# Loading later x tiles already transposed and centring them on GpSimd

## The chip, the cores and the metric

The kernel runs on one core of one Trainium2 chip. The metric is device time in microseconds (us) for one execution, and lower is better. In what follows PE is TensorE, DVE is VectorE, ACT is ScalarE, POOL is GpSimd, and SP is the engine that issues most of the DMAs. A difference of 0.2% is 1.3 us here.

## The reference

A layer normalisation of x (2048 tokens, 512 features) feeds two parallel mixers, whose results are added to x. Cut to what matters:

```python
xn = layernorm(x)                                  # (x - mean) / sqrt(var + 1e-5), per token
# A: linear attention, 32 heads of 16
q, k, v = split(xn @ wqkv)
phi_q, phi_k = [softmax(p), softmax(-p)] of p = q @ w_phi and of p = k @ w_phi, per head
o = phi_q (phi_k^T v) / (phi_q phi_k^T 1)
# B: gated MLP over the sequence
z = gelu(xn @ w_in);  z1, z2 = halves of z;  z2 = layernorm(z2)
out = x + o @ wo + (z1 * (w_sp @ z2 + b_sp)) @ w_out
```

## The kernel before

The 2048 tokens are 16 tiles of 128. Products run as three passes of float32r parts (`mm3`, lines 51 to 53: high times high, high times low, low times high), so every operand is split into a high part (ACT rounds it, line 43) and a rest (DVE subtracts, line 47).

The change lies in the first stage, about the first 217 us. For each tile `s` the stage does this:

1. `fetch(s)` has SP load the tile, tokens on the partitions (`xt`, line 168, 256 KB). Five such buffers are used in turn, and the blocks of `w_in` (`wst_`, line 179) use the same five.
2. `stats(s)`: DVE takes mean and variance (lines 234 and 236). POOL makes the negative mean `nm` (line 237) and the reciprocal deviation `r_x` (lines 84 and 85).
3. `center(s)`: ACT adds `nm` to the tile, one value per partition (line 242).
4. `transposed(s)`: PE transposes the tile in four blocks into a PSUM tile `pt` (line 248), so that features lie on the partitions.
5. `split_x`: ACT and DVE split `pt` into `xT[s]` (lines 43 and 47).
6. PE multiplies `xT[s]` by the weights: V (`proj`, evicted to `v` by ACT, line 257), K and Q (`proj`, read by DVE, lines 103 to 113, with an exponential on ACT, line 110), and the first half of the gated MLP (`zps`, evicted to `z1f` by ACT, line 139).
7. `add_kv`: DVE scales K's features `e` (line 269), POOL issues a DMA that adds them into `zacc` (line 270), and PE adds to the K-V product (`kvps`, line 273). Q's features go to DRAM (`e_d`, line 265, a DMA that POOL issues).

`proj` and `pt` share four PSUM buffers, `zps` has two. K's `e` has two buffers. Each engine runs its own instructions strictly in order; the order is set when the program is built, by a scheduler that takes instructions as they become ready in its own simulated time. So an edit to a step can move instructions of other steps. Tiles 0 to 2 are handled by lines written out in a fixed order ahead of the loop, and tiles 3 to 15 by `centered(s + 2)` in the loop.

An input `x_t` that holds x with each tile transposed already exists, and this kernel does not read it.

After the first stage come the second half of the gated MLP (to about 290 us), the product with `w_sp` (`g`), and a last stage with the output projections; the change does not touch their code.

Of the kernel before, what the change touches and what calls it, by code (L numbers as in the profile page):

```python
# [10 lines left out]
F32 = mybir.dt.float32  # L11
F32R = mybir.dt.float32r
AF = mybir.ActivationFunctionType
ALU = mybir.AluOpType
# [4 lines left out]
P = 128  # L19
S, D, H, DH, FH = 2048, 512, 32, 16, 688  # L20
NT = S // P
ND = D // P
# [13 lines left out]
def mixer(ctx: ExitStack, tc: tile.TileContext, x, x_t, wv, wqkT, phi_bd, wo, w_in, wst, b_r, w_out, out):  # L36
    nc = tc.nc
    pe, act, dve, pool, sp = nc.tensor, nc.scalar, nc.vector, nc.gpsimd, nc.sync


    def round_h(eng, h, src):
        if eng is act:
            return act.activation(h, src, AF.Copy).ins  # L43
        return eng.tensor_copy(h, src).ins

    def rest_l(l, src, h, eng=None):
        return (eng or dve).tensor_tensor(l, src, h.bitcast(F32), op=ALU.subtract).ins  # L47
# [18 lines left out]
    dram = ctx.enter_context(tc.tile_pool(name="dram", bufs=1, space=DRAM))  # L66
# [2 lines left out]
    u_d = dram.tile([NT, P, FH + REM], F32, name="u_d")  # L69
    kvT_d = dram.tile([P, D], F32, name="kvT_d")  # L70
    zb_d = dram.tile([P, NF], F32, name="zb_d")

    ident = cst.tile([P, P], F32, name="ident")
    make_identity(nc, ident)
# [6 lines left out]
    def rstd_of(mv, r, stats=None):  # L81
        if stats is not None:
            dve.bn_aggr(mv, stats)
        pool.tensor_scalar_add(mv[:, 1:2], mv[:, 1:2], EPS_LN)
        pool.tensor_tensor(r, mv[:, 1:2], mhalf, op=ALU.pow)
# [36 lines left out]
    def zproj(ps, s, w, order=(0, 1)):  # L122

        if ps in (za, kv_ps_p):
            p = [ps.tile([P, D], F32, tag="z", name="zps") for _ in range(2)]
        else:
            q = ps.tile([P, 2, D], F32, tag="z", name="zps")
            p = [q[:, k] for k in range(2)]
        t = xT[s]
        for k, j in enumerate(order):  # L130
            for c in range(ND):
                cs = slice(c * P, (c + 1) * P)
                mm3(p[k][:, :FC], (t[:, 0, cs], t[:, 1, cs]), (w[j][0][:, c], w[j][1][:, c]), c == 0, c == ND - 1)
        return [(slice(k, k + 1), p[k][:, :FC].unsqueeze(1)) for k in range(2)] if ps in (za, kv_ps_p) else [(slice(0, 2), q[:, :, :FC])]

    def z1_raw(pl, ps, s, bufs):
        z = pl.tile([P, 2, FC], F32, tag="zf", bufs=bufs, name="z1f")
        for k, p in zproj(ps, s, w1):
            act.activation(z[:, k], p, AF.Copy, scale=r_x[:, s:s + 1])
        act.dma_start(z1_d[s], z.rearrange("p a b -> p (a b)"))  # L140
# [20 lines left out]
    with ExitStack() as p0:  # L161
        res = p0.enter_context(left("p0res", 1))
        wk = p0.enter_context(left("p0wk", 2))
        ps = p0.enter_context(psum("p0ps", 4))

        def load_x(s):
            t = wk.tile([P, D], F32, tag="x", bufs=XB, name="xt")
            sp.dma_start(t, x[s * P:(s + 1) * P, :])
            return t
# [15 lines left out]
        def load_rows(src, x_at={}):  # L185
            raw = [stage("wrow") for _ in range(2)]
            parts = [raw[c // 2][:, c % 2, :D] for c in range(ND)]
            for c in range(ND):
                if c in x_at:
                    fetch(x_at[c])  # L190
                sp.dma_start(parts[c], src[c * P:(c + 1) * P, :])
            return parts
# [15 lines left out]
        def load_win(dst, j, stp, tag, bufs):  # L208
            for c in range(ND):
                t = stp.tile([P, D if tag == "x" else FC], F32, tag=tag, bufs=bufs, name="wst_")  # L210
                split_w(dst[0][:, c], dst[1][:, c], w_in[c * P:(c + 1) * P, j * FC:(j + 1) * FC], t[:, :FC])

        def proj(s, wh, wl):
            p = ps.tile([P, D], F32, tag="mm", name="proj")
            for c in range(ND):
                cs = slice(c * P, (c + 1) * P)
                proj.last = mm3(p, (xT[s][:, 0, cs], xT[s][:, 1, cs]), (wh[:, c], wl[:, c]), c == 0, c == ND - 1)
            return p

        xt, v = {}, {}  # L220

        def fetch(s):
            if s < NT:
                xt[s] = load_x(s)

        def split_x(src):
            t = xz.tile([P, 2, FH], F32R, tag="xz", name="xT")
            xT.append(t)
            src = src.rearrange("p a b -> p (a b)")
            return round_h(act, t[:, 0, :D], src), rest_l(t[:, 1, :D], src, t[:, 0, :D])  # L230

        def stats(s):
            st6 = wk.tile([P, 6], F32, tag="st6", name="st6")
            dve.bn_stats(st6, xt[s])
            nm = wk.tile([P, 1], F32, tag="nm", name="nm")
            ins = dve.bn_aggr(mv_x[:, s], st6).ins
            pool.tensor_scalar_mul(nm, mv_x[:, s, 0:1], -1.0)
            rstd_of(mv_x[:, s], r_x[:, s:s + 1])
            return nm, ins

        def center(s, nm):
            return act.activation(xt[s], xt[s], AF.Identity, bias=nm).ins

        def transposed(s):
            xs = xt.pop(s)
            pt = ps.tile([P, ND, P], F32, tag="mm", name="pt")
            for c in range(ND):
                ins = pe.transpose(pt[:, c], xs[:, c * P:(c + 1) * P], ident).ins  # L248
            return pt, ins

        def centered(s):
            center(s, stats(s)[0])
            split_x(transposed(s)[0])

        def proj_v(s):
            v[s] = wk.tile([P, D], F32, tag="v", name="v")
            ins = act.activation(v[s], proj(s, wv_h, wv_l), AF.Copy, scale=r_x[:, s:s + 1]).ins
            return proj.last, ins

        def proj_k(s):  # L260
            return softmax_pair(wk, proj(s, wqk_h[:, 1], wqk_l[:, 1]), "k", r_x[:, s:s + 1])

        def proj_q(s):
            e = softmax_pair(wk, proj(s, wqk_h[:, 0], wqk_l[:, 0]), "q", r_x[:, s:s + 1])
            pool.dma_start(e_d[s], e)

        def add_kv(s, er):
            vs, e = v.pop(s), er[:, :NF]
            dve.tensor_tensor(heads(e), heads(e), bc(er[:, NF:], 2 * H), op=ALU.mult)
            pool.dma_start(zacc, e, accum_op=ALU.add)  # L270
            for m in range(H // 2):
                k = m % 4 * QP
                pe.matmul(kv_acc[k:k + QP, m // 4], vs[:, m * QP:(m + 1) * QP], e[:, m * HP:(m + 1) * HP],  # L273
                          start=s == 0 and m < 4, stop=s == NT - 1, skip_group_check=True)
# [3 lines left out]
        wvr = load_rows(wv, {2: 1})  # L278
        fetch(2)
        wqT = load_rows(wqkT[:D])  # L280
        fetch(3)
        sp.dma_start(bias, b_r)


# [11 lines left out]
        with ExitStack() as queue:  # L296
# [3 lines left out]
            nm, i = stats(0)  # L300
# [9 lines left out]
            nm, i = stats(1)  # L310
# [8 lines left out]
            p = proj(0, wqk_h[:, 1], wqk_l[:, 1])  # L319
# [5 lines left out]
            nm, i = stats(2)  # L325
# [13 lines left out]
                    proj_v(1)  # L339
        n1 = nq = 0  # L340
        for s in range(NT):
            fetch(s + 4)
            er = proj_k(s) if s else ek
            if 0 < s < NT - 2:
                centered(s + 2)
            while nq < (s - 2) * NT // (NT - 3):
                proj_q(nq)
                nq += 1
            add_kv(s, er)
            if s + 2 < NT:  # L350
                proj_v(s + 2)
            if s == 1:
                for j in range(2):
                    load_win(w1[j], j, wk, "x", XB)
            while n1 < s * (NT - LAG) // (NT - 1):
                z1_raw(wk, za, n1, 2)
                n1 += 1
# [18 lines left out]
    def q_fin(et, tmp, zb):  # L376

        e, r, t, w = et[:, :NF], *(et[:, NF + k * 2 * H:NF + (k + 1) * 2 * H] for k in range(3))
        den = et[:, NF + 6 * H:QW]
        dve.tensor_tensor(tmp, e, zb, op=ALU.mult)  # L380
        dve.tensor_reduce(t, heads(tmp), axis=AX.X, op=ALU.add)
        dve.tensor_tensor(t, t, r, op=ALU.mult)
        dve.scalar_tensor_tensor(den, pairs(t, 0), EPS_DEN, pairs(t, 1), op0=ALU.add, op1=ALU.add)
        dve.reciprocal(den, den)
        dve.tensor_tensor(w.rearrange("p (h a) -> p h a", a=2), r.rearrange("p (h a) -> p h a", a=2),
                          den.unsqueeze(2).to_broadcast([P, H, 2]), op=ALU.mult)
        return e, dve.tensor_tensor(heads(e), heads(e), bc(w, 2 * H), op=ALU.mult).ins
# [46 lines left out]
    with ExitStack() as p1:  # L434
# [39 lines left out]
        for s in range(NE):  # L474
            et = load_q(s, tb.tile([P, QW], F32, tag="et", bufs=2, name="et"))
            tmp = zw.tile([P, 4, FC], F32, tag="z2", bufs=2, name="qtmp").rearrange("p a b -> p (a b)")[:, :NF]
            e, _ = q_fin(et, tmp, zb)
# [11 lines left out]
    nb = 0  # L489
# [44 lines left out]
    for s in range(NT):  # L534
        p = zproj((kv_ps_p, zc, zbp, za)[s % 4], s, w2, (0, 1) if s % 2 == 0 else (1, 0))
# [171 lines left out]
    wk = ctx.enter_context(left("cwk", 2))  # L707
# [82 lines left out]
    p = {0: project_u(0, uT.pop(0))}  # L790
# [20 lines left out]
    for i in range(0, NT, 2):  # L811
        if i:
# [3 lines left out]
            with tc.issue_after(lasts[2]):  # L816
                oT, _ = attend(fT)
# [49 lines left out]
```

## Time and profile before

| | |
|---|---|
| median of 3 runs | 654.72 us (654.68 to 655.67) |
| span of the profiled execution | 651.5 us, so 3.2 us of the median lie outside a span like this one; no other time of that execution is given |
| PE busy | 644.0 us (99% of the span) |
| DVE, ACT, POOL busy | 509.3, 279.4 and 96.6 us |
| granted TensorE clock | 1.000 |
| DMA | 98.36 MB, mean 151 GB/s |

Busy time of PE counts from the start of a matmul to its modelled end, and matmuls overlap; the distance from one start to the next is what one costs. In the chain of work that ended last, each piece has its start, its length on the chain and what it is. A list of waits names the waiting instruction first, then what released it, then the total, the number of times and the longest.

### The profile page before, as it was taken

The page shows a single profiled execution, that of the slowest core. Times are in us where ns is not written, and L with a number is a line of the kernel's source. Part 1 is how long each engine was busy: PE and PEld are TensorE (multiplying, and loading weights), DVE is VectorE, ACT ScalarE, POOL GpSimd, SP SyncE. Part 2 cuts the span into 40 slices and gives each one's busy share as a digit, 9 for nine tenths or more (in the row PEclk, how much of TensorE's full clock was granted, in tenths as well). Part 3 has the DMA queues.
Part 4 walks back from the last instruction along what each step waited for, and adds up shares of the span by engine and source line. Part 5 has one row for each costly group of instructions (what it writes and reads, how often), then busy time and mean ns, then how long its engine had stood idle before and what let it go on. Part 6 is the DMA issues. An engine that isn't in the chain of part 4 may idle for free.

```text
span 651.5 us, 10927 instructions
## 1 busy us (share of the span) xinstructions
PE 644.0 (99%) x4163; PEld 580.2 (89%) x4163; DVE 509.3 (78%) x921; ACT 279.4 (43%) x464; POOL 96.6 (15%) x185
## 2 busy tenths in 40 slices
PE   7999999999999999999999999999999999999997
PEld 6888888888888999999999999999999777787885
DVE  4988987998889578989977869678696588989321
ACT  5644334342333438887443434434452432233220
POOL 3332221101101014441010010010100000001000
PEclk9999999999999999999999999999999999999999
DMA  8365344544444951002353352433557867864610
GB/s 307 78 161 138 100 130 103 149 124 113 124 141 144 302 164 65 2 2 78 129 187 128 124 171 89 163 122 115 177 182 269 290 210 265 295 237 165 214 50 32
DMA packets 38884, 98.36 MB, mean 151 GB/s; under 512 B 4688, under 2 KB 6736, under 8 KB 38832
## 3 DMA queue, kind: packets, MB, share of 16 engines
q1 hardware_dynamic: 27632, 56.77, 26.7%
q0 software_dynamic: 8896, 35.26, 17.8%
q10 hardware_dynamic: 2304, 5.64, 2.3%
q8 instruction: 32, 0.52, 0.3%
q14 instruction: 20, 0.16, 0.1%
HBM read 56.37 MB, written 26.61 MB: 127 GB/s over the span
## 4 chain that ended last, share of the span: by engine, by line
PE 97%; DMA 1%; DVE 0%; ACT 0%; SPq 0%; issue 0%; POOL 0%; POOLq 0%
PE g L53 11%; PE g L52 11%; PE g L51 11%; PE proj L53 7%; PE proj L51 7%; PE proj L52 7%; PE zps L53 6%; PE zps L52 6%; PE zps L51 6%; PE pout L51 5%; PE pout L53 5%; PE pout L52 5%; PE po L761 2%; PE kvps L273 1%; PE ptq L749 1%; PE pt L248 1%
## 5 line engine op out<-in xcount | busy, mean ns | idle before, releaser
L53 PE MATMUL g<-B,A 128*128 128x344 f32 x448 | 143.3, 320 | 0.0
L52 PE MATMUL g<-B,A 128*128 128x344 f32 x448 | 143.2, 320 | 0.0
L51 PE MATMUL g<-B,A 128*128 128x344 f32 x448 | 143.2, 320 | 0.0
L51 PEld LDWEIGHTS g<-B,A 128*128 128x128 f32 x448 | 84.2, 188 | 0.0
L53 PEld LDWEIGHTS g<-B,A 128*128 128x128 f32 x448 | 84.2, 188 | 0.0
L52 PEld LDWEIGHTS g<-B,A 128*128 128x128 f32 x448 | 84.1, 188 | 0.0
L47 DVE TENSOR_TENSOR A<-S,A 128x512 fp32r<-128x512 f32 x64 | 43.7, 688 | 33.4 <-ACT A L43 32.5
L43 ACT ACTIVATE A<-S 128x512 fp32r<-128x512 f32 x64 | 40.0, 631 | 58.5 <-PE g L53 36.3
L110 ACT ACTIVATE e<-e,r_x 128x1024 f32<-128x1024 f32 x32 | 36.8, 1152 | 43.8 <-DVE e L109 43.1
L51 PE MATMUL proj<-wqk_h,xT 128*128 128x512 f32 x128 | 51.4, 401 | 0.3 <-ACT wqk_h L43 0.3
L52 PE MATMUL proj<-wqk_l,xT 128*128 128x512 f32 x128 | 50.5, 394 | 1.1 <-DVE wqk_l L47 1.1
L43 ACT ACTIVATE A<-wf 128x512 fp32r<-128x512 f32 x64 | 33.4, 522 | 41.1 <-PE g L53 40.4
L53 PE MATMUL proj<-wqk_h,xT 128*128 128x512 f32 x128 | 50.9, 397 | 0.0
L51 PE MATMUL zps<-w_0h,xT 128*128 128x344 f32 x128 | 41.8, 326 | 0.0
L112 DVE TENSOR_REDUCE sm<-e 128x64 f32<-128x1024 f32 x32 | 38.6, 1208 | 3.3 <-ACT e L110 3.3
L53 PE MATMUL zps<-w_0h,xT 128*128 128x344 f32 x128 | 41.1, 321 | 0.0
L51 PE MATMUL zps<-w_1h,xT 128*128 128x344 f32 x128 | 41.0, 320 | 0.0
L53 PE MATMUL zps<-w_1h,xT 128*128 128x344 f32 x128 | 41.0, 320 | 0.0
L52 PE MATMUL zps<-w_0l,xT 128*128 128x344 f32 x128 | 40.9, 320 | 0.0
L52 PE MATMUL zps<-w_1l,xT 128*128 128x344 f32 x128 | 40.9, 319 | 0.0
L47 DVE TENSOR_TENSOR A<-wf,A 128x512 fp32r<-128x512 f32 x64 | 35.4, 553 | 3.9 <-ACT A L43 3.4
L751 ACT ACTIVATE f<-ptq 128x512 f32<-128x512 f32 x32 | 16.5, 603 | 34.7 <-PE ptq L749 27.8
(193 smaller groups left out, 1439.9 us busy)
## 6 DMA issues: line engine op xcount, KB each, us to landing
wf<-in_wst SPq DMA_DIRECT2D x64, 256.0 KB, 3.4
e_d<-e POOLq DMA_DIRECT2D x16, 544.0 KB, 5.2
et<-e_d SPq DMA_DIRECT2D x16, 544.0 KB, 4.9
zacc<-e POOLq DMA_DIRECT2D x16, 512.0 KB, 4.9
er<-et POOLq DMA_DIRECT2D x12, 512.0 KB, 4.6
u_d<-z1t POOLq DMA_DIRECT2D x16, 368.0 KB, 4.4
u<-u_d SPq DMA_DIRECT2D x15, 368.0 KB, 4.6
z_d<-z1f ACTq DMA_DIRECT2D x16, 344.0 KB, 3.4
```

The costliest lines, as they stand in the source:

```text
L43: return act.activation(h, src, AF.Copy).ins
L47: return (eng or dve).tensor_tensor(l, src, h.bitcast(F32), op=ALU.subtract).ins
L51: pe.matmul(dst, ah, bh, start=start, stop=False)
L52: pe.matmul(dst, ah, bl, start=False, stop=False)
L53: return pe.matmul(dst, al, bh, start=False, stop=stop).ins
L110: act.activation(e, e, AF.Exp, scale=scale)
L112: dve.tensor_reduce(sm, heads(e), axis=AX.X, op=ALU.add)
L248: ins = pe.transpose(pt[:, c], xs[:, c * P:(c + 1) * P], ident).ins
L273: pe.matmul(kv_acc[k:k + QP, m // 4], vs[:, m * QP:(m + 1) * QP], e[:, m * HP:(m + 1) * HP], start=s == 0 and m < 4, stop=s == NT - 1, ski ...
L749: pe.transpose(pt[:, a, k].bitcast(F32R), src, ident_r)
L751: act.activation(f, pt.rearrange("p a k b -> p a (k b)"), AF.Copy)
L761: lasts[3] = pe.matmul(po[g // 2][a * HP:(a + 1) * HP, g % 2], kvT[:, 2 * g + a], fs[g][:, a], start=True, stop=True).ins
```

## The change

Tiles 3 to 15 are no longer centred by ACT and transposed by PE. Each is loaded twice: once as before (for mean and variance alone), and once from `x_t`, transposed, into `xc` (two buffers, 256 KB each). Since a token's mean now belongs to a column and not to a partition, POOL issues a DMA that writes the 128 values of `nm` to a row in DRAM, SP issues a DMA that reads that row back into all 128 partitions (`nb`, two buffers, 64 KB), and POOL adds `nb` to `xc`, 128x512 elements. `split_x` then reads `xc`.

```diff
+    nm_d = dram.tile([NT, P], F32, name="nm_d")
...
-        def centered(s):
-            center(s, stats(s)[0])
-            split_x(transposed(s)[0])
+        xc = {}
+
+        def load_xT(s):
+            if s >= NT:
+                return
+            fetch(s)
+            xc[s] = wk.tile([P, ND, P], F32, tag="xc", bufs=2, name="xc"), wk.tile([P, P], F32, tag="nb", bufs=2, name="nb")
+            sp.dma_start(xc[s][0], x_t[s])
+
+        def center_T(s):
+            if s >= NT:
+                return
+            nm, _ = stats(s)
+            xt.pop(s)
+            t, nb = xc[s]
+            pool.dma_start(nm_d[s:s + 1, :].rearrange("a p -> p a"), nm)
+            sp.dma_start(nb, nm_d[s:s + 1, :].to_broadcast([P, P]))
+            pool.tensor_tensor(t, t, nb.unsqueeze(1).to_broadcast([P, ND, P]), op=ALU.add)
...
-        fetch(3)
+        load_xT(3)
...
-            fetch(s + 4)
+            load_xT(s + 4)
+            if s == 0:
+                center_T(3)
             er = proj_k(s) if s else ek
             if 0 < s < NT - 2:
-                centered(s + 2)
+                split_x(xc.pop(s + 2)[0])
+                center_T(s + 3)
```

The scheduler places the new instructions, and this is seen on three queues. First POOL, about 30 us into the program. Before, `nm_594` is the negative mean of tile 5, `nm_722` that of tile 6, and `e_249` and `e_375` are K's features of tiles 0 and 1:

```order
L237 TENSOR_SCALAR nm_594<-mv_x_76 128x1
L84 TENSOR_SCALAR mv_x_76<-mv_x_76 128x1
L85 TENSOR_TENSOR r_x_77<-mv_x_76,mhalf_73 128x1
L270 DMA zacc_94<-e_249 128x1024
L270 DMA zacc_94<-e_375 128x1024
L237 TENSOR_SCALAR nm_722<-mv_x_76 128x1
```

After, `xc_142`, `xc_328` and `xc_376` are the transposed tiles 3, 4 and 5, `nm_513` is the negative mean of tile 5, and `e_253` K's features of tile 0:

```order
L269 TENSOR_TENSOR xc_142<-xc_142,nb_143 128x512
L238 TENSOR_SCALAR nm_513<-mv_x_77 128x1
L85 TENSOR_SCALAR mv_x_77<-mv_x_77 128x1
L267 DMA nm_d_68<-nm_513 128x1
L86 TENSOR_TENSOR r_x_78<-mv_x_77,mhalf_74 128x1
L269 TENSOR_TENSOR xc_328<-xc_328,nb_329 128x512
L269 TENSOR_TENSOR xc_376<-xc_376,nb_377 128x512
L286 DMA zacc_95<-e_253 128x1024
```

The additions now stand between the statistics and ahead of the DMA into `zacc`, and the mean of tile 5 is taken only behind the addition of tile 3.

Second ACT, at the splits of the first tiles of the loop. Before, `xT_395` and `xT_501` are tiles 3 and 4, `v_342` is V of tile 2, and `e_375` and `e_481` are K's features of tiles 1 and 2:

```order
L43 ACTIVATE xT_395<-pt_390 128x512
L257 ACTIVATE v_342<-proj_343,r_x_77 128x512
L110 ACTIVATE e_375<-e_375,r_x_77 128x1024
L139 ACTIVATE z1f_537<-zps_538,r_x_77 128x344
L43 ACTIVATE w1_1h_112<-wst__455 128x344
L43 ACTIVATE w1_1h_112<-wst__459 128x344
L43 ACTIVATE xT_501<-pt_496 128x512
L242 ACTIVATE xt_463<-xt_463,nm_722 128x512
```

After, `xc_328`, `xc_376`, `xc_482` and `xc_586` are tiles 4 to 7, `e_395` and `e_501` K's features of tiles 1 and 2, and `v_359` and `v_433` V of tiles 2 and 3:

```order
L43 ACTIVATE xT_508<-xc_328 128x512
L43 ACTIVATE xT_612<-xc_376 128x512
L111 ACTIVATE e_395<-e_395,r_x_78 128x1024
L140 ACTIVATE z1f_554<-zps_555,r_x_78 128x344
L273 ACTIVATE v_359<-proj_360,r_x_78 128x512
L111 ACTIVATE e_501<-e_501,r_x_78 128x1024
L140 ACTIVATE z1f_554<-zps_556,r_x_78 128x344
L43 ACTIVATE xT_740<-xc_482 128x512
L141 DMA z1_d_64<-z1f_554 128x688
L43 ACTIVATE xT_838<-xc_586 128x512
L273 ACTIVATE v_433<-proj_434,r_x_78 128x512
```

The splits have moved forward by several tiles: tile 5 is split ahead of the exponential of K of tile 1, and tile 7 ahead of the eviction of V of tile 3.

Third SP, in the same stretch. Before, only loads of x follow each other there; after, `nb_483` and `nb_587` are the broadcasts of tiles 6 and 7, and `xt_1316` and `xt_1444` the plain loads of tiles 13 and 14:

```order
L259 DMA xc_482<-in_x_t 128x512
L259 DMA xc_586<-in_x_t 128x512
L268 DMA nb_483<-nm_d_68 128x128
L169 DMA xt_1316<-in_x 128x512
L169 DMA xt_1444<-in_x 128x512
L268 DMA nb_587<-nm_d_68 128x128
```

A broadcast now stands behind loads that wait for a buffer, and loads of later tiles behind broadcasts that wait for a write to DRAM.

## The prediction

> **What bounds the kernel now.** I read the page first (span, engines, chain), then PE's waits, then the stage windows, then the groups that the change touches.
>
> ```profile
> span 651.5 us, 10927 instructions
> PE 644.0 (99%) x4163; PEld 580.2 (89%) x4163; DVE 509.3 (78%) x921; ACT 279.4 (43%) x464; POOL 96.6 (15%) x185
> PE 97%; DMA 1%; DVE 0%; ACT 0%; SPq 0%; issue 0%; POOL 0%; POOLq 0%
> ```
>
> The chain is PE from end to end. PE's waits and the windows (columns: window, then busy us of PE, PEld, DVE, ACT, POOL, then clock, DMA share, GB/s) say where it is not full:
>
> ```profile
> PE idle L293 <- POOL ident masks.py:199: 1.8, 1, 1.8
> PE proj L52 <- DVE wqk_l L47: 1.1, 1, 1.1
> PE proj L51 <- ACT wqk_h L43: 0.3, 1, 0.3
> ...
> 31.00:60.00 29.00, 29.00 (x233) 24.68 (x233) 25.33 (x42) 14.44 (x22) 9.97 (x20) 1.00 0.53 128
> 60.00:100.00 40.00, 40.00 (x313) 33.39 (x312) 34.25 (x53) 15.86 (x21) 7.99 (x16) 1.00 0.52 138
> 100.00:200.00 100.00, 100.00 (x693) 84.20 (x692) 86.59 (x124) 36.36 (x45) 14.10 (x23) 1.00 0.43 123
> 217.00:240.00 23.00, 23.00 (x142) 22.00 (x141) 14.37 (x28) 12.51 (x24) 0.00 (x0) 1.00 0.84 277
> ```
>
> All of PE's waits are in the start; from 31 us on it has none, at clock 1.00. So work taken off PE there shortens the span one for one, as long as nothing else makes PE wait. DVE is next, at 85 to 87% of the stage that changes.
>
> **What is removed from PE.** The transposes of 13 tiles, four matmuls each. In the chain the first and the last of these 13 pieces, and one with its neighbours:
>
> ```profile
> 30.67 0.44 PE pt L248 x4
> ...
> 177.71 0.44 PE pt L248 x4
> ```
>
> ```profile
> 72.31 0.23 PE proj L53
> 72.55 0.44 PE pt L248 x4
> 72.98 0.16 PE zps L53
> 73.14 0.16 PE zps L51
> ```
>
> ```profile
> L248 PE MATMUL pt<-ident,xt x52: 270/272/273, 30.5 to 177.9; 128*128 128x128 f32 x52
> ```
>
> 52 is 13 times 4. The neighbours keep their steps of 0.23 and 0.16, so no changeover hides around a piece. 13 x 0.44 = 5.7 us. This is the main term, and all of it is on the path.
>
> **What is removed or cheaper elsewhere.** ACT loses 13 centrings, and the splits read SBUF instead of PSUM:
>
> ```profile
> L242 ACT ACTIVATE xt<-xt,nm 128x512 f32<-128x512 f32 x16 | 11.5, 722 | 22.5 <-POOL nm L237 22.5
> L43 ACT ACTIVATE xT<-pt 128x512 fp32r<-128x512 f32 x16 | 9.6, 598 | 21.8 <-PE pt L248 21.8
> L43 ACT ACTIVATE A<-wf 128x512 fp32r<-128x512 f32 x32 | 20.1, 628 | 26.3 <-PE g L53 25.6 <-ACT A L43 0.4 <-DMA wf<-in_wst 0.3
> L47 DVE TENSOR_TENSOR xT<-pt,xT 128x512 fp32r<-128x512 f32 x16 | 10.8, 678 | 2.5 <-ACT xT L43 2.5
> L47 DVE TENSOR_TENSOR A<-wf,A 128x512 fp32r<-128x512 f32 x32 | 22.0, 686 | 2.9 <-ACT A L43 2.8
> ```
>
> ACT is freed 13 x 0.72 = 9.4 us; it is half idle in this stage, so this is worth nothing by itself. The same split from SBUF (`wf`) takes 628 and 686 ns, against 598 and 678 from PSUM: no gain. Also `pt` no longer takes one of the four PSUM buffers, which lets PE run further ahead of DVE. I count that as zero, since PE never waits there.
>
> **What is added.** For each of 13 tiles: one addition on POOL, one tiny DMA issued by POOL, one broadcast and one 256 KB load issued by SP. The nearest rows:
>
> ```profile
> L154 POOL TENSOR_TENSOR mask<-mask 128x128 f32<-128x128 f32 x1 | 0.5, 455 | 0.1
> L76 POOL MEMSET mhalf<- 128x1 f32 x1 | 0.1, 98 | 0.0
> L265 POOL DMA_DIRECT2D e_d<-e x16 | 9.2, 574 | 21.9 <-DVE e L113 8.4 <-issue 5.0 <-DVE e L108 4.2
> ...
> e_d<-e POOLq DMA_DIRECT2D x16, 544.0 KB, 5.2
> xt<-in_x SPq DMA_DIRECT2D x16, 256.0 KB, 4.6
> out<-xr SPq DMA_DIRECT2D x16, 256.0 KB, 2.1
> wst__431<-in_w_in SPq DMA_DIRECT2D x1, 172.0 KB, 2.3
> ```
>
> The addition has four times the elements of the `mask` addition: between 98 + 4 x (455 - 98) ns = 1.53 us and 4 x 455 ns = 1.82 us; I take 1.5, since a fixed part is not repeated. With 0.6 us for the DMA's issue POOL gets 13 x 2.1 = 28 us more, and it is 14 to 34% busy in the windows above. The DMAs add 13 x (256 + 64) KB = 4.2 MB; over the 70 us or so in which the walk below places them that is 60 GB/s, beside the 128 to 138 that are moved at half load. Neither engine is near full.
>
> The landing of the tiny write and of the broadcast is shown nowhere. The nearest rows go from 2.1 us (a 256 KB store) to 5.2 us (the 544 KB that POOL issues). I take 2.7 for the write and 2.2 for the broadcast, nearer the lower end, since the longer times are of more bytes; 4.9 together, 10.4 at the upper end. The Trainium skill, "DMA: Bandwidth & Descriptors", section "Specifications", says that pieces below 512 B make the engine read, modify and write; the write here is of 4-byte pieces, and no run here shows one. By that rule its time would lie higher in this range.
>
> **Is a tile ever late?** The order sets the question: ACT holds V of tile 3 (`v_433`) behind the split of tile 7, and ACT waits in order. `v_433` frees the PSUM buffer that V of tile 5 takes on PE. Durations for the walk:
>
> ```profile
> L110 ACT ACTIVATE e<-e,r_x 128x1024 f32<-128x1024 f32 x32 | 36.8, 1152 | 43.8 <-DVE e L109 43.1 <-ACT z1f L139 0.7
> L257 ACT ACTIVATE v<-proj,r_x 128x512 f32<-128x512 f32 x16 | 10.9, 682 | 10.4 <-PE kvps L273 10.3
> 42.45 0.58 PE kvps L273 x32
> 43.03 0.43 PE proj L53
> ```
>
> PE: from 30.7 us, where tile 3's transposes were, it has ahead of V of tile 5 five products of V, K and Q (60 `proj` matmuls x 0.23), the first half of the gated MLP for two tiles (48 x 0.157) and two `kvps` (0.58 each, and the `proj` behind one takes 0.43 instead of 0.23): 13.9 + 7.5 + 1.6 = 23.0. So V of tile 5 is due at 53.7.
>
> POOL and SP, by the prices above: tile 3's mean is written by 23, broadcast by 25, added by 26.7. POOL takes tile 5's mean only then: written by 30, broadcast by 32; its `xc` is loaded when tile 3's split has freed the buffer, and lands by 35; added by 36.5, split by 38.5. That frees tile 7's buffer; its broadcast is issued at about 43.5 behind loads of x, and lands by 45.7; POOL has means and a DMA in between and adds at 46.6 to 48.1. ACT splits (0.6) and evicts V of tile 3 (0.7): 49.4. That is 4.3 us ahead of need. Tiles 8 to 11 come out the same way at 3 to 6 us each, one to four us ahead. So at my prices PE never waits, and the whole 5.7 remain. If the cover is gone, the evictions of V and `z1f` are late next, and PE waits on PSUM.
>
> With both landings at 5.2 us, tile 7 is added at 52.6, just in time; tile 8, whose mean POOL takes behind tile 6, is 1.9 us late at the eviction of V of tile 4; tiles 10 and 11 make `z1f` another 3.7 late. That is 5.7 us: exactly the gain.
>
> **At the start**, the two extra 256 KB loads stand ahead of the first `w_in` block; its row on the chain:
>
> ```profile
> 15.31 2.27 DMA wst__431<-in_w_in
> 19.93 0.66 PE pt L248 x4
> ```
>
> ```profile
> GB/s 307 78 161 138 100 130 103 149 124 113 124 141 144 302 164 65 2 2 78 129 187 128 124 171 89 163 122 115 177 182 269 290 210 265 295 237 165 214 50 32
> ```
>
> Two loads at the 307 GB/s of the first slice cost up to 1.7 us, but DVE now takes tile 2's mean ahead of that block's rest, which returns 0.5 to 1.0. I count zero, with 0.5 either way. Behind the stage, PE is full too (217 to 240 above), so a gain is passed on to the end.
>
> **Sum.** 651.5 - 5.7 = 645.8 us of span; on the median of the runs, whose 3.2 us outside the span don't change, 654.7 - 5.7 = 649.0.
>
> **One contention, weighed.** POOL's and DVE's rows at one place:
>
> ```profile
> 46.38 1.23 DVE L269 TENSOR_TENSOR e<-e 128x1024 f32<-128x1024 f32 x1
> ...
> 46.54 1.14 POOL L84 TENSOR_SCALAR mv_x<-mv_x 128x1 f32<-128x1 f32 x1
> ```
>
> POOL's smallest operation took 1.14 us and ended with DVE's. So the two seem to shut each other out, and an addition of 1.5 us could hold DVE in turn. Six additions fall in 31 to 60 us; at 0.6 us each they take 3.7 us, which is all the idle time that DVE has there (29.0 - 25.3). The Trainium skill, "SBUF — State Buffer", section "Who interferes with whom", says that a DVE instruction with two SBUF inputs and a GpSimd instruction that reads SBUF exclude each other for a whole instruction. By that rule the split and the scaling of `e` are held; the trace agrees with the 1.14 us.
>
> **The rivals.**
> - Full gain (above), 648.2 to 650.5: 0.50.
> - Part of it lost: DVE held as just worked out and PE losing up to 3.7 us, or landings between my prices and the upper end: 650.5 to 653.4. Chance 0.24.
> - The round trip eats the gain, landings near 5.2 us each: 653.4 to 656.0, no change that a measurement could tell. Chance 0.12.
> - Slower: the round trip of the mean, in ACT's order. It decides from 10.4 us for write and broadcast together; each further us is paid again at tiles 8, 10, 12 and 14, whose splits stand ahead of evictions, so at 11.5 us about 5.7 + 4 x 1.1 = 10 us of waits: 659. Against it speaks that it needs more than twice my price. Chance 0.14.
> - That the transposes remain is excluded: only those of tiles 0 to 2 are left in the program.
>
> **Numbers.** Faster 0.74, same 0.12, slower 0.14. The likeliest is 649.0. The range 648.2 to 656.0 leaves out the slower case and little below the full gain.
>
> **What would show it.** Right: 12 transposes left, no PE wait behind 31 us, the span near 646, POOL's addition 1.5 us, the broadcast's landing near 2. Wrong: ACT's `xT` waiting on POOL's `xc` and PE on ACT's `v` or `z1f` between 38 and 80 us; or a write to `nm_d` that lands after more than 5 us.

## The result, and the profile after

The changed kernel takes 704.62 us (median; 702.49 to 708.76) beside 654.7 us for the kernel before (654.5 to 655.67): a ratio of 1.0768, 95% interval 1.073 to 1.0806. It is slower by 50 us. The forecast of 649.0 us was wrong, and so was its range.

The head of the page after, and the engines' line of the chain:

```profile
span 700.8 us, 10907 instructions
PE 648.1 (92%) x4111; PEld 580.3 (83%) x4111; DVE 509.1 (73%) x921; ACT 269.7 (38%) x451; POOL 120.5 (17%) x211
PEclk9989785999999999999999999999999999999999
PE 78%; DMA 1%; DVE 1%; issue 0%; ACT 0%
```

The chain can be followed back only to 139.5 us here, so its shares say nothing of the stage before that. The 52 transposes are gone (4163 matmuls before, 4111 now), and yet PE is busy for longer, and no longer for the whole span. PE's longest waits after (what waited, what released it, total us, times, longest):

```profile
PE zps L51 <- ACT z1f L140: 18.0, 2, 16.3
PE proj L51 <- ACT v L273: 15.9, 3, 9.7
PE proj L51 <- ACT xT L43: 5.3, 1, 5.3
PE proj L51 <- DVE e L110: 4.5, 3, 2.6
```

The windows after show where (window, busy us of PE, PEld, DVE, ACT and POOL, then clock, DMA share, GB/s):

```profile
20.00:40.00 20.00, 14.69 (x66) 11.93 (x65) 11.89 (x23) 8.66 (x17) 7.69 (x13) 0.85 0.68 99
...
60.00:80.00 20.00, 10.31 (x99) 7.99 (x99) 10.76 (x20) 2.27 (x4) 7.60 (x14) 0.74 0.43 93
80.00:100.00 20.00, 14.56 (x93) 11.79 (x91) 9.66 (x16) 4.46 (x6) 7.48 (x12) 0.91 0.80 92
100.00:120.00 20.00, 4.03 (x13) 3.64 (x14) 7.34 (x11) 4.79 (x7) 9.06 (x16) 0.57 0.30 58
120.00:140.00 20.00, 16.36 (x104) 13.08 (x103) 9.94 (x15) 4.56 (x7) 7.60 (x6) 1.00 0.80 151
...
160.00:180.00 20.00, 20.00 (x150) 16.19 (x149) 18.96 (x29) 5.81 (x7) 3.38 (x5) 1.00 0.44 122
20.00:160.00 140.00, 96.06 (x623) 78.01 (x622) 80.99 (x131) 36.82 (x56) 48.10 (x75) 0.87 0.58 106
```

From 20 to 160 us PE stands idle for 140 - 96.1 = 43.9 us, where before it had no wait at all. The granted clock is lower there too: 0.57 in the 20 us in which PE works for 4.03. Three matmuls, the last ahead of a wait of 5.3 us and the first two behind it (start, us, instruction, idle time before it and what released it):

```profile
30.07 0.40 PE L53 MATMUL proj<-wv_h,xT 128*128 128x512 f32 x1
35.77 0.79 PE L51 MATMUL proj<-wv_h,xT 128*128 128x512 f32 x1 [5.31 <-ACT xT L43]
36.37 0.63 PE L52 MATMUL proj<-wv_l,xT 128*128 128x512 f32 x1
```

After each of PE's four longest waits (5.2 to 16.3 us) the matmuls of 128x512 take 0.63 us in place of 0.39, for 3 to 5 us; after the waits of 1.8 and 2.6 us they don't. From 160 us on PE is full again. In the 80 to 100 us row the DMA engines are busy for 0.80 of the time and move 92 GB/s; at 0.80 again, from 120 to 140 us, they move 151. Busy, then, is not the same as moving.

The waits behind PE's, and the DMAs of the first 260 us (KB each, median us to landing):

```profile
ACT xT L43 <- POOL xc L269: 73.6, 11, 13.5
POOL xc L269 <- DMA xc<-in_x_t: 29.2, 6, 11.8
POOL xc L269 <- DMA nb<-nm_d: 20.5, 2, 11.4
POOL nm L238 <- DMA nm_d<-nm: 19.4, 4, 8.3
...
xc<-in_x_t SPq DMA_DIRECT2D x13, 256.0 KB, 5.4
nb<-nm_d SPq DMA_DIRECT2D x13, 64.0 KB, 5.0
nm_d<-nm POOLq DMA_DIRECT2D x13, 0.5 KB, 8.3
wst__464<-in_w_in SPq DMA_DIRECT2D x1, 172.0 KB, 8.8
```

The write of 512 bytes takes longer than the loads of 256 KB (over the whole run 7.2 to 14.6 us). Five of the eight blocks of `w_in` in this stage take 4.2 to 8.8 us; before, six took 2.2 or 2.3 and the other two 4.1 and 4.8. POOL itself waits for the write four times: the buffer of `nm` is free for a new mean only when the old one has landed. One such place, first on POOL and then on ACT (start, us, instruction, idle time before it and what released it):

```profile
103.51 0.23 POOL L238 TENSOR_SCALAR nm<-mv_x 128x1 f32<-128x1 f32 x1 [8.31 <-DMA nm_d<-nm]
103.72 0.64 POOL L267 DMA_DIRECT2D nm_d<-nm  x1
104.37 0.59 POOL L86 TENSOR_TENSOR r_x<-mv_x,mhalf 128x1 f32<-128x1 f32 x1
104.91 1.27 POOL L269 TENSOR_TENSOR xc<-xc,nb 128x512 f32<-128x512 f32 x1
...
106.22 0.63 ACT L43 ACTIVATE xT<-xc 128x512 fp32r<-128x512 f32 x1 [13.51 <-POOL xc L269]
```

An addition stands in POOL's order behind a mean that waits 8.3 us for a write; ACT waits 13.5 us in order for that addition; meanwhile it evicts neither V nor `z1f`. PE's wait of 16.3 us for a `z1f` lasts over this split and the next, for which ACT waits another 8.0.

### The profile page after: what moved, and what is told of

The parts are those of the page before. It is cut to its first block, busy times and chain, and to the rows that moved or that the text cites. A ratio compares the mean times of both kernels' runs of the same rounds, so it can differ in the third digit from the quotient of the medians.

```text
span 700.8 us, 10907 instructions
## 1 busy us (share of the span) xinstructions
PE 648.1 (92%) x4111; PEld 580.3 (83%) x4111; DVE 509.1 (73%) x921; ACT 269.7 (38%) x451; POOL 120.5 (17%) x211
## 3 DMA queue, kind: packets, MB, share of 16 engines
q0 software_dynamic: 9312, 35.27, 18.2%
## 4 chain that ended last, share of the span: by engine, by line
PE 78%; DMA 1%; DVE 1%; issue 0%; ACT 0%
PE g L53 10%; PE g L51 10%; PE g L52 10%; PE pout L51 5%; PE zps L52 5%; PE zps L51 5%; PE zps L53 5%; PE pout L52 5%; PE pout L53 5%; PE proj L51 4%; PE proj L53 4%; PE proj L52 4%; PE po L780 2%; PE ptq L768 1%; PE pout L794 1%; DMA u<-u_d 1%
## 5 line engine op out<-in xcount | busy, mean ns | idle before, releaser
L47 DVE TENSOR_TENSOR A<-S,A 128x512 fp32r<-128x512 f32 x64 | 43.9, 688 | 27.3 <-ACT A L43 26.7
L51 PE MATMUL proj<-wqk_h,xT 128*128 128x512 f32 x128 | 52.9, 414 | 11.0 <-ACT v L273 6.2
L53 PE MATMUL proj<-wqk_h,xT 128*128 128x512 f32 x128 | 51.9, 405 | 0.0
L47 DVE TENSOR_TENSOR xT<-xc,xT 128x512 fp32r<-128x512 f32 x13 | 9.3, 715 | 43.7 <-ACT xT L43 43.7
L51 PE MATMUL proj<-wv_h,xT 128*128 128x512 f32 x64 | 26.8, 419 | 15.0 <-ACT v L273 9.7
```

The costliest lines, as they stand in the source:

```text
L51: pe.matmul(dst, ah, bh, start=start, stop=False)
L53: return pe.matmul(dst, al, bh, start=False, stop=stop).ins
```

## The experiments

The kernel before ran beside each group: 655.05 us beside the first four, 654.82 beside the next four, 654.9 beside the last four.

**1 to 4: take the trip apart.** In `no_trip` no mean goes through DRAM; POOL adds a tile `nb0` of zeros, so the tiles are not centred.

```diff
+    nb0 = w1_pool.tile([P, P], F32, name="nb0")
+    pool.memset(nb0, 0.0)
...
-            pool.dma_start(nm_d[s:s + 1, :].rearrange("a p -> p a"), nm)
-            sp.dma_start(nb, nm_d[s:s + 1, :].to_broadcast([P, P]))
```

> Leaves out the write of the mean to DRAM and its broadcast: POOL adds a tile of zeros, so the x tiles are not centred. All else (the second load from x_t, POOL's 13 additions, no transposes) stays. If the round trip through DRAM is the cause: 648.5 to 651, PE without waits after the start, clock 1.00. If POOL's additions shutting out DVE, the extra 256 KB loads, or the splits moved forward in ACT's order are the cause: still near 700.

Measured: 649.77 us, ratio 0.9927 (0.9913 to 0.9941). The page, PE's longest wait behind the start, the addition and the second load:

```profile
span 647.8 us, 10863 instructions
PE 639.0 (99%) x4111; PEld 575.5 (89%) x4111; DVE 509.1 (79%) x921; ACT 270.5 (42%) x451; POOL 115.5 (18%) x199
PE ptu L657 <- DMA u<-u_d: 1.2, 1, 1.2
L269 POOL TENSOR_TENSOR xc<-xc,nb 128x512 f32<-128x512 f32 x13 | 18.2, 1406 | 13.0 <-DMA xc<-in_x_t 10.3 <-DVE e L110 2.7
xc<-in_x_t SPq DMA_DIRECT2D x13, 256.0 KB, 3.1
```

So the additions, the second load and the missing transposes together are as forecast, and what was lost comes with the two DMAs that this kernel leaves out. The order is not quite the changed kernel's, since each kernel is scheduled anew; but ACT's splits stand even further forward here (six of the 13 ahead of the third `v`, against three), so splits that stand early are not what cost 50 us. PE's busy time beside the changed kernel's, 648.1 - 639.0 = 9.1 us for the same 4111 matmuls, goes with the slower clock: the slow matmuls behind the four longest waits, counted by the distance to the next start, make an estimated 8.6. The span's other 43.9 us of 53.0 are idle time.

`write_only` is `no_trip` with the write and without the broadcast (nobody reads what is written):

```diff
 # on top of no_trip
+            pool.dma_start(nm_d[s:s + 1, :].rearrange("a p -> p a"), nm)
```

> The write of nm to DRAM (128 pieces of 4 bytes, issued by POOL) stays, the broadcast is left out and POOL adds zeros. If the write holds up the DMA engines for everyone: 665 to 695, with the loads of x_t and w_in landing 3 us and more later than without it. If it is only slow for the one who waits for it: below 655, since only POOL's next nm but one waits for it.

Measured: 690.87 us, 1.0548 (1.0518 to 1.0579). Its waits of PE and its DMAs:

```profile
PE proj L51 <- DVE e L110: 20.3, 4, 8.3
PE proj L51 <- ACT v L274: 8.7, 2, 8.5
...
xc<-in_x_t SPq DMA_DIRECT2D x13, 256.0 KB, 10.2
nm_d<-nm POOLq DMA_DIRECT2D x13, 0.5 KB, 10.4
...
wst__473<-in_w_in SPq DMA_DIRECT2D x1, 172.0 KB, 13.6
```

The write alone costs 41.1 us over `no_trip`. Loads that SP issues, on another queue, land as late as the write. They don't only start late: between 20 and 45 us the packets of SP's queue take 87% of the DMA engines' time here and move 3.05 MB (in `no_trip` 60% for 4.65 MB), while POOL's queue, with the writes alone, shows 0.3%. POOL also waits for the landing itself, since `nm` has two buffers (32.4 us in five waits). The loss comes by both ways, the late loads and POOL's wait: on the chain of this run stand a block of `w_in` with 13.6 us and a wait for such a write with 18.3. No run parts them.

`bcast_only` has the broadcast and not the write; it reads a row of x, so nothing is waited for ahead of it:

```diff
-            pool.dma_start(nm_d[s:s + 1, :].rearrange("a p -> p a"), nm)
-            sp.dma_start(nb, nm_d[s:s + 1, :].to_broadcast([P, P]))
+            sp.dma_start(nb, x[s * P:s * P + 1, :P].to_broadcast([P, P]))
```

> The broadcast stays, but reads 128 values of x (a row that is in DRAM from the start), and nothing is written: the wrong row is added. If the broadcast alone is dear (128 reads of one 512-byte row, 5 us each in the trace): 655 to 670. If the write is what counts: below 653.

Measured: 654.35 us, 0.9993 (0.9978 to 1.0009): 4.6 us over `no_trip`, between the two cases expected. The broadcast lands in 3.4 us. Write and broadcast singly make 41.1 + 4.6 = 45.7 of the 704.62 - 649.77 = 54.9 us; the other 9.2 appear only with both. That the broadcast then has to wait for the write is the likely reason, but no run shows it, and the changed kernel's own times spread over 6.3 us.

`diag_row` brings the mean into all partitions without DRAM: POOL makes a diagonal of it, PE multiplies it by ones, ACT copies the product.

```diff
-            pool.dma_start(nm_d[s:s + 1, :].rearrange("a p -> p a"), nm)
-            sp.dma_start(nb, nm_d[s:s + 1, :].to_broadcast([P, P]))
+            dg = wk.tile([P, P], F32, tag="dg", name="dg")
+            pool.tensor_scalar(dg, ident, nm, None, op0=ALU.mult)
+            pn = ps.tile([P, D], F32, tag="mm", name="pn")
+            pe.matmul(pn[:, :P], ones, dg, start=True, stop=True)
+            act.activation(nb, pn[:, :P], AF.Copy)
```

> No DRAM: POOL scales the identity's rows by nm, one PE matmul of ones with that (128x128, 0.11 us by the fold rows) makes the mean row in all partitions in PSUM, ACT copies it to SBUF as nb, POOL adds it. PE saves 13 x (0.44 - 0.11) = 4.3 us. If the round trip is the cause: 650 to 652, faster than before. If POOL's additions or the order are: above 660.

Measured: 652.8 us, 0.9965 (0.9953 to 0.9976). The whole computation, with three engines in place of two DMAs, is 0.35% faster than before, though a little above what was expected. It stands 3.0 us above `no_trip`, 0.23 us for each tile: its product, which PE runs in two passes (26 matmuls for 13 products) and which was priced at 0.11, and what goes with it.

**5 to 7: what of the write is dear?** `write_only` could be slow because its pieces have 4 bytes, because GpSimd issues it, or because its 128 pieces lie together. The first two kernels are `write_only` with one thing changed; the third is the first with wider pieces.

```diff
 # w_spread: each 4-byte piece to a row of its own, 512 bytes apart
-    nm_d = dram.tile([NT, P], F32, name="nm_d")
+    nm_d = dram.tile([NT, P, P], F32, name="nm_d")
...
+            pool.dma_start(nm_d[s, :, 0:1], nm)
```

> Write only, no broadcast, POOL adds zeros, as in write_only; but each of the 128 pieces of 4 bytes goes to a row of its own, 512 bytes apart, instead of one 512-byte row. If the pieces hold each other up because they meet in one row: 650 to 656, and loads of w_in land in 2 to 4 us again. If pieces of 4 bytes are dear wherever they go: 685 to 695 as write_only.

```diff
 # w_sp: the write of write_only, issued by SP
+            sp.dma_start(nm_d[s:s + 1, :].rearrange("a p -> p a"), nm)
```

> Write only, as in write_only, but SP issues the write instead of POOL. If POOL's queue is to blame: 650 to 656. If it is the pieces: 680 to 700 again.

```diff
 # w_wide: 512 bytes from each partition, to a row of its own (nm_d as in w_spread)
+            nw = wk.tile([P, P], F32, tag="nw", name="nw")
+            pool.tensor_scalar(nw, nb0, nm, None, op0=ALU.add)
+            pool.dma_start(nm_d[s], nw)
```

> Write only, and each of the 128 partitions writes 512 bytes (its mean 128 times over, 64 KB in all) to a row of its own; POOL makes that tile, 0.3 to 0.7 us more per tile. If small pieces or one shared row are to blame: 650 to 656 though 128 times the bytes are written. If any write of 128 pieces from POOL holds up the others: near 690.

| | time, us | ratio (95%) | write lands in |
|---|---|---|---|
| `write_only` | 690.87 | 1.0548 (1.0518 to 1.0579) | 10.4 us |
| `w_sp` | 699.25 | 1.0677 (1.0655 to 1.0698) | 9.4 us |
| `w_spread` | 649.63 | 0.9919 (0.9899 to 0.9939) | 3.3 us |
| `w_wide` | 649.17 | 0.9912 (0.9892 to 0.9932) | 3.2 us |

The DMAs of `w_sp`, then those of `w_spread`, then the write of `w_wide`:

```profile
xc<-in_x_t SPq DMA_DIRECT2D x13, 256.0 KB, 10.5
nm_d<-nm SPq DMA_DIRECT2D x13, 0.5 KB, 9.4
wst__469<-in_w_in SPq DMA_DIRECT2D x1, 172.0 KB, 16.6
```

```profile
xc<-in_x_t SPq DMA_DIRECT2D x13, 256.0 KB, 3.6
nm_d<-nm POOLq DMA_DIRECT2D x13, 0.5 KB, 3.3
wst__469<-in_w_in SPq DMA_DIRECT2D x1, 172.0 KB, 2.7
```

```profile
nm_d<-nw POOLq DMA_DIRECT2D x13, 64.0 KB, 3.2
```

Neither the size of a piece nor the issuer decides. The same 128 pieces of 4 bytes, laid 512 bytes apart, cost nothing in the time and land as soon as 128 pieces of 512 bytes do. It is where they lie to each other: `write_only` and `w_spread` have the same 9312 packets on POOL's queue, and ACT takes its splits, exponentials and evictions of this stage in the same order in both.

**8: the change with a cheap write.** `row_write` is the whole change, but PE turns the mean into a row first, so that the write is one piece of 512 bytes:

```diff
-            pool.dma_start(nm_d[s:s + 1, :].rearrange("a p -> p a"), nm)
+            pn = ps.tile([P, D], F32, tag="mm", name="pn")
+            pe.transpose(pn[:1, :P], nm, ident)
+            nr = wk.tile([1, P], F32, tag="nr", name="nr")
+            act.activation(nr, pn[:1, :P], AF.Copy)
+            pool.dma_start(nm_d[s:s + 1, :], nr)
             sp.dma_start(nb, nm_d[s:s + 1, :].to_broadcast([P, P]))
```

> The whole change with its round trip, but PE first turns nm into a row (one transpose, 0.11 to 0.25 us), ACT copies it to SBUF, and POOL writes one piece of 512 bytes; the broadcast reads it back as before. x is centred. If the 128 small pieces are the cause and not the trip itself: 653 to 660 (broadcast alone gave 654, the trip adds latency, PE pays 2 to 3). If the trip's latency through DRAM is the cause: above 675.

Measured: 664.53 us, 1.0142 (1.0123 to 1.0161): 40 us below the changed kernel, but above what was expected. Its DMAs and its longest waits:

```profile
nb<-nm_d SPq DMA_DIRECT2D x13, 64.0 KB, 3.4
nm_d<-nr POOLq DMA_DIRECT2D x13, 0.5 KB, 3.4
...
POOL xc L273 <- DMA nb<-nm_d: 44.9, 10, 7.6
PE kvps L293 <- DVE e L289: 3.5, 1, 3.5
PE proj L51 <- ACT nr L270: 3.1, 1, 3.1
```

Both landings are now inside the forecast's bounds, 6.8 us together, and PE still waits: the broadcast is what POOL's additions wait for, ten times. So the way through DRAM is too long here even though neither of its transfers is slow.

**9 and 10: how far apart, and does anybody have to read it?** `w_64` is `w_spread` with the pieces 64 bytes apart:

```diff
-    nm_d = dram.tile([NT, P], F32, name="nm_d")
+    nm_d = dram.tile([NT, P, 16], F32, name="nm_d")
```

> Write only, POOL adds zeros, the pieces of 4 bytes 64 bytes apart (8 KB per tile; they were 4 bytes apart in write_only, 512 apart in w_spread). If pieces disturb each other only inside one unit of 64 bytes or less: about 650. If inside one row of 512 bytes: 8 pieces still meet, 653 to 670. If the whole neighbourhood counts: near 690.

Measured: 649.79 us, 0.9927 (0.9909 to 0.9946). Its write:

```profile
nm_d<-nm POOLq DMA_DIRECT2D x13, 0.5 KB, 2.9
```

At 64 bytes the pieces no longer disturb each other, at 4 they do; distances between were not tried.

`before_write` is the kernel before, with the same 13 writes added and nothing else:

```diff
-            center(s, stats(s)[0])
+            nm, _ = stats(s)
+            pool.dma_start(nm_d[s:s + 1, :].rearrange("a p -> p a"), nm)
+            center(s, nm)
```

> The kernel before, with one write of nm (128 pieces of 4 bytes into one row of 512 bytes) added for each of tiles 3 to 15, which nobody reads. If the writes hold up every DMA engine for 5 to 8 us each: the loads of x and w_in land late here too, and the time is 658 to 685. If only the change's dependence of x tiles on its own write and loads makes them dear: 654 to 657.

Measured: 681.61 us, 1.0413 (1.0394 to 1.0432), 26.7 us for 13 writes that nobody reads, 2.05 us each. Here too the write and the loads beside it are slow:

```profile
nm_d<-nm POOLq DMA_DIRECT2D x13, 0.5 KB, 9.0
wst__453<-in_w_in SPq DMA_DIRECT2D x1, 172.0 KB, 7.5
wst__457<-in_w_in SPq DMA_DIRECT2D x1, 172.0 KB, 9.0
```

Nobody reads the values, but POOL waits for their landing here too before it reuses `nm` (18.4 us in three waits). In the chain of this run two such waits, of 10.8 and 8.0 us, follow each other from 51 us on, and ahead of them stand two blocks of `w_in` that take 8.1 and 8.4 us. How the time would come out with more buffers of `nm`, so that only the late loads are left, was not tried.

**11 and 12: a better kernel, and the broadcast.** `diag_r` is `diag_row` with the diagonal and the ones in float32r, so that PE needs one pass:

```diff
+    ones_r = w1_pool.tile([P, P], F32R, name="ones_r")
+    pool.tensor_copy(ones_r, ones)
...
-            dg = wk.tile([P, P], F32, tag="dg", name="dg")
+            dg = wk.tile([P, P], F32R, tag="dg", name="dg")
...
-            pe.matmul(pn[:, :P], ones, dg, start=True, stop=True)
+            pe.matmul(pn[:, :P], ones_r, dg, start=True, stop=True)
```

> diag_row with the ones and the scaled identity as float32r, so that PE's product is one pass instead of two: PE saves 13 x 0.12 = 1.5 us against diag_row's 652.8: 650.5 to 652, and faster than before by 0.5 to 0.7%. If PE's part were not what bounds diag_row: 652.8 again.

Measured: 651.02 us, 0.995 (0.9936 to 0.9963), faster than both kernels. PE's largest waits in it lie at the start and, 0.8 us, in a late stage:

```profile
PE idle L314 <- POOL ident masks.py:199: 1.8, 1, 1.8
PE proj L52 <- DVE wqk_l L47: 1.1, 1, 1.1
PE ptu L662 <- DMA u<-u_d: 0.8, 1, 0.8
```

For each tile it has the same kinds of steps on PE and ACT as `row_write` (one short PE operation, one copy), without the two DMAs; so the trip through DRAM, with the order that the scheduler makes for it, costs `row_write` about 664.53 - 651.02 = 13.5 us. Of these the broadcast alone would explain 4.6 (above). The rest, about 9, is as much as the 9.2 that were left in the changed kernel, but the two orders differ, and which of the steps on the way makes these 9 us was not tried.

`bcast_rows` is `bcast_only` with 128 different rows read in place of one:

```diff
-            sp.dma_start(nb, x[s * P:s * P + 1, :P].to_broadcast([P, P]))
+            sp.dma_start(nb, x[s * P:(s + 1) * P, :P])
```

> As bcast_only (nothing written, wrong values added), but the 128 partitions read 128 different rows of 512 bytes instead of one and the same. If reads of one row meet like the writes do, bcast_only's 4.6 us over no_trip vanish: 649.5 to 651. If they come from 13 more loads of 64 KB as such: 654 again.

Measured: 653.04 us, 0.998 (0.9963 to 0.9997), against 0.9993 (0.9978 to 1.0009) for `bcast_only`. The landing differs, 2.0 us here and 3.4 from a single row, but the times can't be told apart. 653.04 - 649.77 = 3.3 of the broadcast's 4.6 us remain with different rows; so most of it seems to come with 13 more loads as such. What they hold up is left open.

## Why the prediction was wrong

Two steps failed: the landing of the write, which was sized too small (2.7 us, measured 8.3), and above all what the write does to the other transfers, which was put at nothing (`write_only`, with no trip to wait for, loses 41.1 us).

**What bounds the kernel, and the 5.7 us on PE: right.** `no_trip` comes out at 649.77 us where 649.0 was forecast, 5.3 us under the kernel before. A gain on PE in this stage passes through to the end, and so, for the same reason, does a loss.

**POOL's addition, 1.5 us: right.** It took 1406 ns in `no_trip` and 1375 on average in the changed kernel, a little under the range of 1.53 to 1.82. (13 x 2.1 us on POOL are 27, not 28, and 6 x 0.6 are 3.6, not 3.7; neither matters.) **DVE held by it: no price.** DVE's busy time is 509.1 us in `no_trip` and 509.3 before, and PE waits for DVE there only as before, 1.1 us at the start. The rule of the Trainium skill, "SBUF — State Buffer", section "Who interferes with whom", would have cost time; single instructions are longer (one addition of `no_trip` took 2.1 us, one split on DVE 1.6), but PE doesn't lose by it.

**The landings, "2.7 for the write and 2.2 for the broadcast": failed.** They measured 8.3 and 5.0 us, 13.3 together, above the upper end of 10.4. The bounds were the nearest rows by kind of queue and by bytes, 2.1 to 5.2 us. Bytes were a weak guide already in the trace before, where a load of 8 KB (`bias`) landed in 4.9 us and a write of 256 KB (`kvT_d`) in 6.4. What sets this write's time is neither: it is 128 pieces that lie 4 bytes apart, and no row of the trace before has such a pattern. The sentence of the Trainium skill that was weighed there ("DMA: Bandwidth & Descriptors", section "Specifications", on pieces under 512 B) points upward, as it came out, but the size alone is not the cause: pieces of 4 bytes at a distance landed in 3.3 and 2.9 us, pieces of 512 in 3.2. The measurement decides, and it asks for the distance. Whether neighbouring pieces meet in such a read, modify and write is not shown.

**"Neither engine is near full" and the prices of all other transfers: the step that cost most.** The sum took each transfer's duration from the trace before, and treated the write as 0.5 KB that take nothing from the others. In `write_only` the loads of `xc` took 10.2 us where `no_trip` has 3.1, and blocks of `w_in` up to 13.6 where `no_trip` has none above 3.5 in the same stage. A loss of 41 us for a DMA of 512 bytes, 13 times over, was in none of the cases; in the kernel before, the same 13 writes cost 27 us with no other change.

**The walk, "tile 7 is 4.3 us ahead of need": its frame held, its margin did not.** It named the waits that appeared (ACT's `xT` on POOL's `xc`, PE on ACT's `z1f` and `v`), and its slower rival, given 0.14, had the way by which a delay reaches PE. It did not have the cause: with 13.3 us for the two landings its own rule gives 5.7 + 4 x (13.3 - 10.4) = 17 us of waits, PE lost 44, and `write_only` loses 41.1 us with no round trip at all. The walk left out three things: POOL waits for the write itself, to reuse `nm` (19.4 us in all); the loads come late as well (29.2 us of POOL's waits, more than the 20.5 for `nb`); and a PE that waits is slower afterwards. `row_write` shows that the walk was too lenient in any case: with landings of 3.4 and 3.4 us, which by the walk cost a part of 5.7 us at most, the trip cost about 13.5.

**The clock: not foreseen.** The clock was taken to be 1.00 because PE was full. A wait is paid twice, as idle time (43.9 us) and as slower matmuls after it (9.1). The Trainium skill, "TensorE: Matmul & The Clock Gate", section "What's actually happening", says that the clock halves after an idle window of some 3.4 us; the granted 0.57 where PE worked 4.03 us of 20 agrees with that.

## What to carry to other kernels

Before a small vector is sent through DRAM, look at how its bytes lie there: one value from each of 128 partitions into one row is 128 pieces of 4 bytes side by side, and here that held up the loads of other queues, where the same values 64 bytes apart cost nothing. To turn a column of values into a row on all partitions, a diagonal and a product with ones on PE took no DMA and one short matmul, and was the only form of this change that kept the whole computation and gained. When a forecast rests on a transfer whose pattern no row of the trace shows, the nearest row by bytes is no bound, and the chance should go to the case in which it is far off, above all where a kernel is bound by one engine that nothing may interrupt.

## What the runs showed that was not expected

- A DMA of 128 pieces of 4 bytes, 4 bytes apart, landed after 10.4 us (8.2 at the least); 64 or 512 bytes apart it took 2.9 and 3.3 us.
- Such a write delays transfers of other queues by about as much as it takes itself: loads of 256 KB landed in 10.2 us in place of 3.1. It is no better when SP issues it in POOL's place (699.25 and 690.87 us), so it doesn't hang on POOL or its queue. The Trainium skill, "DMA: Bandwidth & Descriptors", section "Back-pressure in remote DMA", says of transfers between cores that stalled writes stall the other queues of their DMA engine; the delayed loads fit that, though this write goes to DRAM. At what distance between 4 and 64 bytes the pieces stop disturbing each other, and in what they meet, was not settled.
- Reading one row of 512 bytes into 128 partitions landed in 3.4 us, reading 128 rows in 2.0.
- The addition on POOL, 128x512 with two inputs, took 1.4 us and cost DVE no busy time that the profile shows (509.1 us with it, 509.3 before).
